# A routed two-layer MLP behind an FFT mixing: where on ScalarE's queue the rows of a later block are asked for

## The chip, the cores and the metric

The kernel runs on one core of one Trainium2 chip. The metric is the time on the device in microseconds (us) of one launch, and the median over several runs is compared. Everything is float32.

## The reference

The input `x` has 8 batches of 2496 rows with 256 columns. Two operations follow each other.

```python
X = np.fft.rfft(x, axis=1)                       # mixing along the rows of a batch
y = np.fft.irfft(X * (filt_r + 1j * filt_i)[None], n=2496, axis=1)

tokens = y.reshape(8 * 2496, 256)                # 19968 rows
expert = token_ids * 2654435761 % 8              # which of 8 experts a row goes to
for e in range(8):
    out[expert == e] = np.maximum(tokens[expert == e] @ w1[e], 0) @ w2[e]
```

`w1[e]` is 256 x 1024 and `w2[e]` is 1024 x 256. The result has one row of 256 for each token, in the order of the tokens.

## The kernel before, in words

**Mixing.** A transform of length 2496 is done as 39 x 64, in products with tables (`wf_t`, `d_t`, `e_t`, `wi_t`) on TensorE (PE). Between the two halves of a transform the data go through DRAM, because rows and columns have to change places. For one batch: `stage1` makes products `pa` (L267), which ScalarE (ACT) copies out of PSUM (L269), and writes `d1` to DRAM (`d<-mid`, L297); `load2` reads it again (`mid<-d`, L303, on the queue of SyncE, SP); `forward` makes `pb` (L312), which VectorE (DVE) multiplies with the filter; `back` makes `pc` (L335), ACT copies it (L338) and writes `d2` (L342, on ACT's queue); `load4` reads it (`t<-d`); `stage3` makes `pd` (L267), ACT copies it (L269), and GpSimd (POOL) scatters the rows to a DRAM buffer `xs` in the order of their experts (L433). The products of the mixing share four PSUM buffers; each is free again when its copy out of PSUM is done.

**Routing.** The rows in `xs` lie in 85 places of 256 rows, called blocks here; every block belongs to one expert. For block `i` the function `step(i)` issues, in this order: the sums of the weights of block `i + 1` on POOL (L877), the scatter of the results of block `i - 1` on POOL (L1014), the first product with its relus (`up`), a load of weights (`w1` of block `i + 2`, on SP), the transposes (DVE L855, which read the rows `xg` of block `i + 1`) and sums for block `i + 1`, the second product (`down`), and another load of weights (`w2` of block `i + 2`).

`up` works by a scheme with seven products of half size instead of eight. Its partial sums lie in the PSUM banks `a`, `b` and `c` (`up_a`, `up_b`, `up_c`, L887). In the order of the code: the first product goes to bank `a`, and ACT copies it into the quarter `h21` of the hidden layer `ht` (L898). After it come products in `b` and `c`; DVE adds them up (L894); ACT applies the relu to the four quarters (L891) as they get ready, the last of them at the end of `up`. `down` makes 32 products `dps` (L922) which read `ht`. After every eighth of them there is a spot, in which pieces of the mixing may be issued.

**How they are interleaved.** A block needs only those batches whose rows it can hold. There are five stages, `STAGES = (2, 3, 4, 6, 8)`: blocks 0 to 9 hold rows of the first two batches alone, blocks 10 to 19 of the first three, blocks 20 to 29 of the first four, blocks 30 to 49 of the first six, and from block 50 on of all. So mixing of batches 2 to 7 is laid between the steps 0 to 49: a list of pieces, each with a due time in steps, written out by hand. `run_until` and `spot` issue all pieces that have become due. From step 50 (`WS`) another form of the step is used, `late_step`, which the change doesn't touch. [...]

**Asking for rows.** `load(j)` (from L835) fetches the rows of block `j` into `xg` with four transfers of 64 KB and their places in the output into `no` with a fifth, of 1 KB; from block 2 on all five are issued on ACT's queue (L844). There are two buffers for `xg`. `ask` decides when a block is fetched:

```python
def ask(i, sooner=False):
    j = asked[0]
    if j <= i + 2 or (sooner and j == i + 3 < NT and stage_of[j] == stage_of[j - 1]):
        if j < NT:
            load(j)
            asked[0] += 1
```

It is called twice in a step: once in `up`, for block `i + 2`, and once in the first spot of `down`, with `sooner`, for block `i + 3`. The second may not cross into a new stage, since the first block of a stage must wait for the scatters of the batches that come with it. So the call in the spot has nearly always done the work already when the next step's `up` comes to its own call. The call in `up` loads something only at the start (step 0 loads block 2) and at the first block of each further stage: step 8 loads block 10, step 18 block 20, step 28 block 30, step 48 block 50.

[...]

Of the kernel before, what the change touches and what calls it, by code (L numbers as in the profile page):

```python
# [125 lines left out]
def kernel(  # L126
# [319 lines left out]
    def weights(i, which):  # L446

        if i >= NT:
            return
        if i >= 2 and which == 0:  # L450
            ws[i] = ws[i - 2][0:2]
        eng, kw = nc.sync, {}
        if which == 0:
            ws[i].append(eng.value_load(chunk_i[0:1, 0, i:i + 1], min_val=0, max_val=E - 1))
            if i >= 2:
                ws[i].append(eng.value_load(chunk_i[0:1, 1, i:i + 1], min_val=0, max_val=1))
        e = ws[i][2]
        if i >= 2:
            kw = {"cond": ws[i][3]}
        if which == 0:  # L460


            for f in (slice(0, F // 2), slice(F // 2, F)) if i < 2 else (slice(0, F),):
                eng.dma_start(out=ws[i][0][:, :, f],
                              in_=moe_w1[bass.ds(e, 1)].rearrange("one (p dp) f -> p (one dp) f", p=P)[:, :, f], **kw)
        else:
            eng.dma_start(out=ws[i][1], in_=moe_w2[bass.ds(e, 1)].rearrange("one (fp p) d -> p (one fp) d", p=P), **kw)
            if WS <= i < NSURE:
                eng.dma_start(out=late["t2"][i % 2].rearrange("p k f c -> p (k f c)"),
                              in_=t2_dram[bass.ds(e, 1)].rearrange("one p k -> p (one k)"), **(kw if i >= WS + 2 else {}))  # L470
# [280 lines left out]
    def chain(k):  # L751

        for step, j in ((Batch.turn2, k + 1), (Batch.back_c, k - 2), (Batch.forward, k)):
            if 0 <= j < N_2:
                step(first, j)
# [79 lines left out]
    def load(i):  # L835

        g = gath.tile([P, TB // 32, C // 4], F32, name=f"xg_{i}", tag="xg")
        no = nums.tile([P, 2], I32, name=f"no_{i}", tag="no")
        rows = xs[tiles[i] * TB:(tiles[i] + 1) * TB, :]
        moves = [(g[32 * q:32 * q + 32, :, :], rows[:, 64 * q:64 * q + 64].rearrange("(a t) c -> t a c", t=32))  # L840
                 for q in range(4)]
        moves.append((no[:].bitcast(F32), rows[:, C:C + 1].rearrange("(h p) c -> p (h c)", p=P)))
        for k, (to, src) in enumerate(moves):
            ld = (nc.sync if i < 2 and (i or k < 3) else nc.scalar).dma_start(out=to, in_=src)  # L844
            for b in range(STAGES[stage_of[i]], B):
                tc.declare_no_dep(ld.ins, group=f"xs_{b}", reason="the tiles of a stage hold tokens of its batches alone")
            if stage_of[i] < G - 1:
                tc.declare_no_dep(ld.ins, group="xs_pad", reason="places without a token lie in the last stage alone")
            tc.add_to_no_dep_group("xs_read", ld.ins)
        xg[i], to_rows[i] = g, no  # L850

    def token_parts(i, to=None):

        xt = work.tile([P, DP, 2, P], F32, name=f"xt_{i}", tag="xt")[:] if to is None else to
        nc.vector.transpose(out=xt.rearrange("p d h (a t) -> p (h a) d t", t=32),  # L855
                            in_=xg[i][:, :, 0:C // 4].rearrange("p a (c d) -> p a d c", d=DP))
        parts[i] = {(h, d): xt[:, d, h, :] for h in range(2) for d in range(DP)}

    def token_sums(i, to=None, which=range(4)):
        x = parts[i]  # L860
        st = parts[i].get("sums", to)
        if st is None:
            st = work.tile([P, 4, P], F32, name=f"st_{i}", tag="st")
        for k in which:
            p, q, op = (((1, 0), (1, 1), OP.add), (0, (0, 0), OP.subtract),
                        ((0, 0), (1, 0), OP.subtract), ((0, 1), 1, OP.subtract))[k]
            p, q = [st[:, v, :] if isinstance(v, int) else x[v] for v in (p, q)]
            nc.vector.tensor_tensor(st[:, k, :], p, q, op=op)
        parts[i]["sums"] = st

    def weight_sums(i, eng=None):

        eng, w1, h = eng or nc.gpsimd, ws[i][0], F // 2
        b11, b12, b21, b22 = [w1[:, d, f * h:f * h + h] for d in range(DP) for f in range(2)]
        t = [tpool[i % 2].tile([P, h], F32, name=f"tw_{i}_{k}", tag=f"tw{k}") for k in range(4)]
        for k, (p, q) in enumerate(((b12, b11), (b22, t[0][:]), (b22, b12), (b21, t[1][:]))):
            eng.tensor_tensor(t[k][:], p, q, op=OP.subtract)  # L877
        sums[i] = t

    def up(i, ht, between=lambda: None):  # L880
        w1, x, st, t = ws[i][0], parts[i], parts[i]["sums"], sums[i]
        ps = {k: banks[k].tile([P, 4, P], F32, name=f"up_{i}_{k}", tag=k) for k in "abc"}
        h11, h12, h21, h22 = [ht[:, h, 4 * f:4 * f + 4, :] for h in range(2) for f in range(2)]

        def product(bank, w, xx, first, fs=range(4)):
            for f in fs:
                nc.tensor.matmul(out=ps[bank][:, f, :], lhsT=w[:, f * P:(f + 1) * P], rhs=xx,  # L887
                                 start=first and f == 0, stop=True, skip_group_check=True)

        def relu(out, in_):  # L890
            nc.scalar.activation(out=out, in_=in_, func=AF.Relu)  # L891

        def plus(out, bank, other):
            nc.vector.tensor_tensor(out, ps[bank][:], other, op=OP.add)  # L894

        h = F // 2
        product("a", w1[:, 0, 0:h], x[0, 0], True)
        nc.scalar.copy(out=h21, in_=ps["a"][:])  # L898
        between()
        product("b", t[1], st[:, 1, :], True)  # L900
        plus(h12, "b", h21)
        product("c", t[0], st[:, 0, :], True)
        plus(h22, "c", h21)
        product("a", w1[:, 1, 0:h], x[0, 1], False, (0, 1))
        product("b", t[2], st[:, 2, :], False)
        plus(h22, "b", h22)
        relu(h22, h22)
        product("a", w1[:, 1, 0:h], x[0, 1], False, (2, 3))
        relu(h11, ps["a"][:])
        product("c", w1[:, 1, h:], st[:, 3, :], False)  # L910
        plus(h12, "c", h12)
        relu(h12, h12)
        product("b", t[3], x[1, 1], False)
        plus(h21, "b", h21)
        relu(h21, h21)
# [95 lines left out]
    def store(i, halves=range(2)):  # L1011
        o = rows[i]
        for h in halves:
            st = nc.gpsimd.indirect_dma_start(  # L1014
                out=out[:], out_offset=bass.IndirectOffsetOnAxis(ap=to_rows[i][:, h:h + 1], axis=0),
                in_=o[:, h, :], in_offset=None, bounds_check=N - 1, oob_is_err=False)
            tc.declare_no_dep(st.ins, group="out_rows", reason="distinct rows")
            tc.add_to_no_dep_group("out_rows", st.ins)
# [9 lines left out]
# [8 lines that stand above are left out]
    def spot(i, k):  # L1036
        if k == 0:
            ask(i, True)
        if k < 3:
            run_until(i + .7 + .1 * k)  # L1040

    def run_until(t):
        while main and main[0][0] < t:
            main.pop(0)[1]()

    def late_step(i):
        ht = work.tile([P, 2, FP, P], F32, name=f"ht_{i}", tag="ht")
        store(i - 1, (1,))
        if i + 1 < NSURE:
            weight_sums(i + 1)  # L1050
        store(i - 1, (0,))
        both(i, ht)

    def step(i):
        if i >= WS:
            late_step(i)
            return
        ht = work.tile([P, 2, FP, P], F32, name=f"ht_{i}", tag="ht")
        if i + 1 < NSURE:
            weight_sums(i + 1)  # L1060
        if i > 0:
            store(i - 1)
        up(i, ht, lambda: ask(i))
        weights(i + 2, 0)
        if i + 1 < NSURE:
            token_parts(i + 1)
            token_sums(i + 1)
        run_until(i + .6)
        down(i, ht, lambda k: spot(i, k))
        weights(i + 2, 1)  # L1070
        run_until(i + 1)
# [59 lines left out]
```

## Time and profile before

| | us |
|---|---|
| median of 3 runs | 1452.11 |
| lowest and highest of these | 1450.68 and 1458.1 |
| the profiled execution | 1424.24 |
| its span in the trace | 1422.5 |
| PE busy | 1373.4 (97%) |
| DVE busy | 890.2 (63%) |
| POOL busy | 830.3 (58%) |
| ACT busy | 416.6 (29%) |
| DMA moved, mean over the span | 196 GB/s |

The profile is one execution on the chip. "Busy" leaves out the instructions that issue DMAs, so an engine whose queue stands at a DMA issue counts as idle. "Idle before, releaser" is the time in which an engine did nothing ahead of an instruction, and what ended it. The chain of waits is followed back from the last instruction: at each step to what released it. The granted clock (PEclk) is the share of its full clock that TensorE got. The profiled execution took 27.87 us less than the median of the runs without a profile.

The requests that the change moves and the copy L898 ahead of them, by the trace of before (us from the start of the span):

| step | copy L898 starts | xg issued from, for | no issued | first relu L891 after it | fetched block |
|---|---|---|---|---|---|
| 0 | 143.96 | 144.18, 5.53 | 151.47 | 151.92 | 2 |
| 8 | 302.80 | 303.17, 1.82 | 305.02 | 306.65 | 10 |
| 18 | 494.07 | 494.68, 5.07 | 500.75 | 501.18 | 20 |
| 28 | 687.25 | 687.54, 1.97 | 689.55 | 691.11 | 30 |
| 48 | 1011.71 | 1012.02, 1.84 | 1013.90 | 1015.70 | 50 |

### The profile page before, as it was taken

To read this page: it belongs to the slowest core of one execution; us is meant where nothing else is said; L and a number is where in the kernel's file an instruction comes from. 1 tells how busy PE (TensorE), PEld (TensorE's weight loads), DVE (VectorE), ACT (ScalarE), POOL (GpSimd) and SP (SyncE) were. 2 spreads that over 40 slices of the span, in tenths; PEclk is the share of its full clock that TensorE was granted. 3 is DMA by queue.
4 is the path that set the end of the run, shared out by engine and by line. 5 is a ranking of instruction groups with operands and counts; after the bars stand their busy time and mean duration, and the time that the engine had idled before them with its cause. 6 is when DMAs were issued, how large, how long until landed. Compare 5 with 4: busy or idle time off the path is not lost.

```text
span 1422.5 us, 26307 instructions
## 1 busy us (share of the span) xinstructions
PE 1373.4 (97%) x9398; PEld 1273.3 (90%) x9398; DVE 890.2 (63%) x1636; ACT 416.6 (29%) x760; POOL 830.3 (58%) x736
## 2 busy tenths in 40 slices
PE   7898999999999999999999999999999999999997
PEld 7776888989888988889999899999999999999997
DVE  7773575575556566445665477657766776676775
ACT  4554122223232223232222222222222222222222
POOL 6167243844665565578533587788855566555563
PEclk9999899999999999999999999999999999999999
DMA  8677765757987698888755785887742526261611
GB/s 222 206 235 216 212 218 121 260 192 245 269 270 224 183 284 264 261 262 273 241 167 131 219 258 170 235 242 235 254 138 68 190 62 199 46 218 42 215 46 35
DMA packets 244505, 278.33 MB, mean 196 GB/s; under 512 B 125171, under 2 KB 213670, under 8 KB 234948
## 3 DMA queue, kind: packets, MB, share of 16 engines
q1 hardware_dynamic: 95149, 179.33, 40.2%
q10 hardware_dynamic: 129303, 52.69, 15.4%
q0 software_dynamic: 19920, 44.59, 8.9%
q8 instruction: 77, 1.26, 0.4%
q14 instruction: 56, 0.46, 0.1%
HBM read 293.65 MB, written 86.15 MB: 267 GB/s over the span
## 4 chain that ended last, share of the span: by engine, by line
PE 86%; DMA 8%; DVE 3%; issue 1%; ACT 1%; ACTq 0%; SPq 0%; POOLq 0%; POOL 0%; DVEq 0%
PE dps L922 22%; PE up_b L887 9%; PE up_a L887 6%; PE up_c L887 6%; PE pd L267 5%; PE pb L312 4%; PE dnc L949 4%; PE dnb L949 4%; PE dna L949 4%; PE upc L944 4%; PE upa L944 4%; PE pc L335 3%; PE pa L267 3%; DMA t<-d 2%; PE upe L944 2%; PE upb L944 2%
## 5 line engine op out<-in xcount | busy, mean ns | idle before, releaser
L922 PE MATMUL dps<-wts,ht 128*128 128x256 f32 x1600 | 370.9, 382 | 6.1 <-ACT ht L891 6.1
L922 PEld LDWEIGHTS dps<-wts,ht 128*128 128x128 f32 x1600 | 304.7, 192 | 50.6 <-ACT ht L891 7.3
L1014 POOL DMA_INDIRECT out_dram<-osb,no x158 | 165.2, 1046 | 219.2 <-DVE osb L956 137.8
L433 POOL DMA_INDIRECT xs<-o,sidx x176 | 177.0, 1006 | 168.7 <-ACT o L269 73.3
L877 POOL TENSOR_TENSOR tw<-wts 128x512 f32<-128x512 f32 x158 | 205.1, 1298 | 116.0 <-DMA wts<-in_moe_w_dram 92.4
L877 POOL TENSOR_TENSOR tw<-wts,tw 128x512 f32<-128x512 f32 x158 | 206.1, 1305 | 6.2
L894 DVE TENSOR_TENSOR ht<-up_b,ht 128x512 f32<-128x512 f32 x150 | 103.7, 691 | 114.6 <-PE up_b L887 91.2
L891 ACT ACTIVATE ht<-ht 128x512 f32<-128x512 f32 x150 | 94.3, 630 | 188.8 <-DVE ht L894 164.9
L322 DVE TENSOR_TENSOR z<-pb,filt 64x512 f32<-64x512 f32 x160 | 110.2, 689 | 30.9 <-PE pc L335 28.9
L927 DVE COPY osb<-dps 128x512 f32<-128x512 f32 x50 | 34.6, 691 | 150.2 <-PE dps L922 149.7
L887 PE MATMUL up_a<-xt,wts 128*128 128x128 f32 x800 | 115.3, 277 | 9.1 <-DVE xt L855 4.9
L887 PEld LDWEIGHTS up_a<-xt,wts 128*128 128x128 f32 x800 | 105.9, 193 | 12.7 <-DVE xt L855 5.3
L887 PE MATMUL up_b<-st,tw 128*128 128x128 f32 x800 | 107.4, 278 | 2.7 <-DVE ht L894 1.8
L887 PEld LDWEIGHTS up_b<-st,tw 128*128 128x128 f32 x800 | 98.1, 193 | 4.9 <-issue 3.7
L953 ACT ACTIVATE ht<-ht 128x512 f32<-128x512 f32 x90 | 56.6, 630 | 122.1 <-DVE ht L956 75.8
L894 DVE TENSOR_TENSOR ht<-up_c,ht 128x512 f32<-128x512 f32 x100 | 69.0, 690 | 37.2 <-PE up_c L887 32.4
L338 ACT COPY mid<-pc 128x512 f32<-128x512 f32 x60 | 35.0, 584 | 154.8 <-PE pc L335 91.5
L267 PE MATMUL pd<-t,wi_t 120*117 120x256 f32 x320 | 77.5, 385 | 2.6 <-DMA t<-d 2.6
L318 DVE TENSOR_TENSOR y<-pb,filt 128x512 f32<-128x512 f32 x80 | 55.1, 689 | 37.8 <-PE pb L312 35.6
L269 ACT COPY o<-pd 117x512 f32<-117x512 f32 x80 | 45.0, 585 | 104.4 <-DMA xg<-xs 45.4
L312 PE MATMUL pb<-mid,d_t 128*128 128x256 f32 x280 | 74.1, 388 | 1.1 <-DVE z L322 1.1
L898 ACT COPY ht<-up_a 128x512 f32<-128x512 f32 x50 | 29.3, 587 | 150.6 <-PE up_a L887 120.7
(210 smaller groups left out, 2466.1 us busy)
## 6 DMA issues: line engine op xcount, KB each, us to landing
wts<-in_moe_w_dram SPq DMA_DIRECT2D x162, 1024.0 KB
xg<-xs ACTq DMA_DIRECT2D x321, 64.0 KB
mid<-d SPq DMA_DIRECT2D x70, 256.0 KB
d<-mid ACTq DMA_DIRECT2D x60, 256.0 KB
d_t<-t2s SPq DMA_DIRECT2D x15, 1024.0 KB
e_t<-t2s SPq DMA_DIRECT2D x15, 1024.0 KB
x<-in_x_dram SPq DMA_DIRECT2D x39, 312.0 KB
t<-d SPq DMA_DIRECT2D x12, 960.0 KB
```

The costliest lines, as they stand in the source:

```text
L267: nc.tensor.matmul(out=ps[0:cols * H, k, :], lhsT=w[:], rhs=src[:, 2 * i + k, :], start=True, stop=True)
L312: nc.tensor.matmul(out=ps[:, i, :], lhsT=d_t[:, s, :], rhs=rhs, start=True, stop=True)
L322: nc.vector.tensor_tensor(out=z[b], in0=ps[a], in1=f_t[1][64 * hi:64 * hi + 64, s1:s1 + 2, :], op=OP.mult)
L433: st = nc.gpsimd.indirect_dma_start(out=xs[:], out_offset=bass.IndirectOffsetOnAxis(ap=index, axis=0), in_=rows, in_offset=None, bounds_ch ...
L877: eng.tensor_tensor(t[k][:], p, q, op=OP.subtract)
L887: nc.tensor.matmul(out=ps[bank][:, f, :], lhsT=w[:, f * P:(f + 1) * P], rhs=xx, start=first and f == 0, stop=True, skip_group_check=True)
L891: nc.scalar.activation(out=out, in_=in_, func=AF.Relu)
L894: nc.vector.tensor_tensor(out, ps[bank][:], other, op=OP.add)
L922: nc.tensor.matmul(out=ps[:, h, :], lhsT=ht[:, h, fp, :], rhs=w2[:, fp, :], start=(fp == 0), stop=(fp == FP - 1))
L944: nc.tensor.matmul(out=ps[:, f, :], lhsT=w[:, f * P:(f + 1) * P], rhs=xx, start=first and f == 0, stop=True, skip_group_check=True)
L949: nc.tensor.matmul(out=ps[:, 0, :], lhsT=a[:, f, :], rhs=b[:, f, :], start=first and f == 0, stop=True, skip_group_check=True)
L1014: st = nc.gpsimd.indirect_dma_start(out=out[:], out_offset=bass.IndirectOffsetOnAxis(ap=to_rows[i][:, h:h + 1], axis=0), in_=o[:, h, :], i ...
```

## The change

The parameter `between` of `up` goes away, and with it the call of `ask` behind the copy L898. `step` calls `ask(i)` itself when `up` has been issued. On ACT's queue the five transfers of a request so stand behind the four relus of `up` and ahead of whatever the mixing issues on ACT next. Instructions below line 898 up to the call move up by one line: `dps` is L921 in the changed kernel, `DVE L894` is L894 still, and the copy L898 stays at its number.

```diff
-    def up(i, ht, between=lambda: None):
+    def up(i, ht):
...
         product("a", w1[:, 0, 0:h], x[0, 0], True)
         nc.scalar.copy(out=h21, in_=ps["a"][:])
-        between()
         product("b", t[1], st[:, 1, :], True)
         plus(h12, "b", h21)
...
-        up(i, ht, lambda: ask(i))
+        up(i, ht)
+        ask(i)
         weights(i + 2, 0)
```

## The prediction

> **What bounds the kernel now.** I begin with the page's chain of waits and its row for the product that follows the relus. The columns of the row are busy time, mean ns of one, then PE's idle time just ahead of it and what ended it.
>
> ```profile
> PE 86%; DMA 8%; DVE 3%; issue 1%; ACT 1%; ACTq 0%; SPq 0%; POOLq 0%; POOL 0%; DVEq 0%
> L922 PE MATMUL dps<-wts,ht 128*128 128x256 f32 x1600 | 370.9, 382 | 6.1 <-ACT ht L891 6.1
> ```
>
> PE sets the end, and all of the 6.1 us that it ever waited ahead of dps was for ACT's relus. The waits say how often (total us, times, longest), and what held ACT itself:
>
> ```profile
> PE dps L922 <- ACT ht L891: 6.1, 2, 3.1
> ACT ht L891 <- DMA xg<-xs: 14.0, 3, 7.4
> ACT mid L338 <- DMA xg<-xs: 26.0, 6, 9.0
> ```
>
> The 6.1 us are two waits, not fifty. They lie in step 0 and step 18. ACT's timeline at step 0 and step 18 shows them (start, length, what, idle time before):
>
> ```profile
> 143.96 0.59 ACT L898 COPY ht<-up_a 128x512 f32<-128x512 f32 x1 [6.35 <-PE up_a L887]
> 144.18 5.53 ACTq L844 DMA_DIRECT2D xg<-xs  x4
> 151.47 0.40 ACTq L844 DMA_DIRECT2D no<-xs  x1
> 151.92 0.63 ACT L891 ACTIVATE ht<-ht 128x512 f32<-128x512 f32 x1 [7.37 <-DMA xg<-xs]
> ...
> 494.68 5.07 ACTq L844 DMA_DIRECT2D xg<-xs  x4
> 500.75 0.38 ACTq L844 DMA_DIRECT2D no<-xs  x1
> ```
>
> The relu stands behind the request in ACT's order, so it waits till the fifth transfer (`no`) is issued. PE's timeline has dps at 153.09 after 3.12 us idle, and at 502.35 after 3.00 us. Then the granted clock halves; by windows (last three columns: PEclk, DMA share, GB/s):
>
> ```profile
> 150.00:152.00 2.00, 0.00 (x0) 0.00 (x0) 1.93 (x5) 0.08 (x1) 0.00 (x0) 1.00 0.34 70
> ...
> 152.00:154.00 2.00, 0.91 (x2) 0.82 (x3) 0.37 (x2) 2.00 (x4) 0.00 (x0) 0.52 0.59 133
> 154.00:156.00 2.00, 2.00 (x6) 1.55 (x6) 0.00 (x0) 0.07 (x1) 0.00 (x0) 0.50 1.02 317
> 158.00:160.00 2.00, 2.00 (x9) 1.69 (x8) 0.00 (x0) 0.00 (x0) 0.00 (x0) 0.78 0.93 285
> ```
>
> The third place to look is after the second request of a stage, asked in `spot`, which is not moved. At step 8/9:
>
> ```profile
> 312.27 0.33 ACTq L297 DMA_DIRECT2D d<-mid  x1
> 314.37 5.09 ACTq L844 DMA_DIRECT2D xg<-xs  x4
> 320.83 0.38 ACTq L844 DMA_DIRECT2D no<-xs  x1
> 321.26 0.59 ACT L338 COPY mid<-pc 128x512 f32<-128x512 f32 x1 [9.02 <-DMA xg<-xs]
> ```
>
> ACT stands still for 9.02 us here, yet PE loses nothing: its pc product, which needs the PSUM buffer that this L338 frees, starts at 322.65. ACT's copy ends at 321.85, so the cover is 0.80 us.
>
> [...] half clock for 6.83 us from 152.1 and 3.41 us from 503.6. [...] 3.00 us did it, and so did one of 2.03 us (at 238.22, half clock for 3.41 us from 240.8), while one of 1.98 us at 789.39 did not. [...] `xg` landed about 1.9 us after its issue at 303.17, but 7.3 us after that at 144.18, where SP's 1.6 MB of d<-mid were under way.
>
> **The change, part by part.** Nothing is added or removed; PE, DVE, POOL and SP keep their order. `ask` inside `up` has something to load only in steps 0, 8, 18, 28 and 48 (blocks 2, 10, 20, 30, 50); elsewhere the spot of the step before has asked. So 25 issues on ACT's queue (5 x 5) go from ahead of four relus to behind them, ahead of the L338, L269, L342, L297 of the mixing. [...] The `xg` moved are read by DVE L855 only in the next step, so their own later landing costs nothing (the cover is the rest of the step, over 10 us).
>
> Clock price: step 0's 32 dps took 10.02 us against 7.07 us in a step at full clock, so its two half-clock windows cost 2.95 us; after 502.35 dps x8, pb x4 and pd x8 took 2.56 + 1.91 + 2.21 against 1.89 + 1.03 + 1.89, so its one window cost 1.87 us.
>
> *Step 0/1.* Gone: 3.12 + 2.95 = 6.07 us. New: the fourth xg_2 now waits for the first of SP's mid<-d (L303, issued from 151.48, landing about 155, estimated), xg_3's for the third to sixth, landing about 157 to 160.4 (issues of 0.95 us each, 7.63 us for 8). ACT would be free at about 161; before it was at 155.6. PE, 6 us earlier, reaches the block-1 product that needs copy L898 (before: 164.09) at about 158.1; the copy takes 0.59 us. So PE waits about 161.3 - 158.65 = 2.65 us, plus one half-clock window, 1.87. Net gain 6.07 - 4.52 = 1.55. Bounds: +6 if mid<-d lands early or the counter frees before; 0 with two windows or a later release.
>
> *Step 8/9.* No PE wait before (the relu waited 3.27 us, but DVE was ready only at 306.62), so nothing to win. Five issues of about 0.46 us (303.17 to 305.5) move ahead of L338, L342, L269, L297: 2.3 us. d<-mid L297 (983 KB, 312.27, landed about 322.0) goes out at about 314.7. In the new allocation `no` of block 11 waits for that very transfer, landing at 324 to 326.6: ACT free at about 325.7 instead of 321.2. pc then starts at about 325.7 + 0.59 + 0.1 = 326.4 instead of 322.65: 3.75 us, plus one window, 1.87: loss 5.62. Bounds: 0 (it lands by 322), 3.75 + 1.2 + 2.95 = 7.9 with two windows and the latest landing.
>
> *Step 18/19.* Gone: 3.00 + 1.87 = 4.87. New: no_20 waits for a t<-d (about 507.5), xg_21 for a mid<-d (about 509) and an x<-in_x (about 511.3). ACT free at about 512 (before 510.31), while PE, 4.9 us earlier, wants the PSUM buffer that L269 frees at about 510: 2.2 us, and a window in about half the cases, 0.9. Net gain 1.75. Bounds: 0 to 4.87.
>
> *Step 28/29 and 48/49.* No PE wait before (relus at 691.11 and 1015.70 had waited for DVE). xg_31 now waits for w1 of block 30 and x<-in_x, ACT free at about 700.2 instead of 696.6, copy L898 at 702.14 slips by 0.9, with 0.6 of slack: loss 0.3 (0 to 2). At 48/49, ACT is free at about 1024.8, just ahead of L898 at 1025.07: 0 (0 to 1).
>
> Sum: 1.55 - 5.62 + 1.75 - 0.3 = **2.6 us slower**. Against the profiled execution of 1424.24 us (span 1422.5 and 1.74 around it) that is 1426.8. The median shown is 1452.11, 27.87 above; I carry the difference over: 1454.7.
>
> **Rivals.**
>
> *A: both waits stay won.* ACT is free whenever it is wanted next; gain 6.07 + 4.87 = 10.9, less 0.3: 1441.5. For it: PE's 3.12 and 3.00 us have one cause, which is gone, and landing times above are estimates. Against it: DMA is at 1.02 of its share at 154 to 158, just when the moved requests go out, and ACT already stood 9.02 us behind one of them. Most that can be won, whatever else.
>
> *B, the other side: ACT is held behind the 983 KB write of step 8.* pc waits for the release, and the clock falls for two windows: 7.9. Steps 1 and 19 get longer waits as well: step 1 nets +0.5 (6.07 - 2.65 - 2.95, a second window), step 19 nets -0.6 (4.87 - 2.2 - 1.4 - 1.87: a release 1.4 us later and the whole window), steps 29 and 49 lose 3 together. Sum 11.0 slower: 1463.1. It decides from the point where no_11 is issued after about 326, 4 us past the old landing of the write. For it: every stretch concerned moves 219 to 322 GB/s, so a write that starts 2.3 us later can end more than 2.3 us later. Against it: its landing is the only long one, and POOL and DVE don't slip.
>
> *C: nothing is gained or lost.* The two waits come back as equal waits a block later, and no_11's counter is free in time: 0, 1452. For it: in both places the release I work out is a transfer's landing, which doesn't depend on where the request stands. Against it: it needs 10.9 us of new waits at steps 1 and 19, where I find 4.52 + 3.1 = 7.6.
>
> **How the numbers follow.** A measurement of this kernel can tell about 0.5% from no change, 7.3 us, so 1444.8 to 1459.4 is "same". My own case has 0.45, of which 0.05 lies beyond 1459.4 (bounds of step 8/9 and 28/29 together); A 0.13; B 0.35[...]; C 0.07. Faster 0.13, same 0.40 + 0.07 = 0.47, slower 0.40. The range reaches from near A to past B: 1443 to 1470. The likeliest: 1455.
>
> **What would show it.** Right: no PE gap ahead of dps (L921 after) at 150 and 499, full clock there; an ACT wait of several us ahead of L338 or L269 near 321 to 326, ended by no, xg or d<-mid, and a new PE gap at pc; a PE gap of 2 to 3 us near 155 to 161 at up_b or up_a for L898 and near 505 to 512 for L269. Wrong: PE gapless through 300 to 330 (step 8/9 costs nothing: then A); the gap at dps still there (C); gaps away from the five places, which I can't derive from the order of the issues.

## The result, and the profile after

The changed kernel takes 1460.97 us (median of 20 runs, 1454.7 to 1471.99), the kernel before 1455.1 us in 20 runs beside it (1449.15 to 1465.71). The ratio is 1.0045 (95% interval 1.0025 to 1.0065): about 6.5 us slower, just short of the 0.5% that the prediction took as the least difference that can be told. A second set of runs of the same kernel gave 1.0043 (1.0023 to 1.0062).

The later sets of runs were each on another chip, and the kernel before takes 1458 and 1453 us on two of these chips and 1423 us on the other two; the profile of before that the prediction was read from (1424.24 us) fits the second kind, the result and the profile of after (1460.99 us) the first, so the two spans, 1422.5 and 1459.2 us, must not be subtracted. Step 0 alone starts 8.9 us later in the trace of after, and nothing ahead of step 0 was changed. For a trace of the first kind I profiled the kernel before again (`e1_before_again`, below); every ratio here is against runs of before in the same set. Both timings of the changed kernel itself are from chips of the first kind.

From the page of after, the chain of waits and the row of the product that follows the relus:

```profile
PE 76%; DMA 9%; DVE 6%; issue 3%; ACTq 1%; ACT 1%; another core or an unknown queue 1%; POOL 1%; SPq 1%; POOLq 0%; DVEq 0%
L921 PE MATMUL dps<-wts,ht 128*128 128x256 f32 x1600 | 368.8, 381 | 0.0
```

The 6.1 us ahead of dps are gone to the last tenth. Two lines from the waits of after (total us, times, longest):

```profile
PE up_a L887 <- ACT ht L898: 10.8, 5, 4.8
ACT mid L338 <- DMA xg<-xs: 39.8, 8, 12.2
```

ACT stands longer behind requests ahead of L338, 39.8 us where it was 26.0. The 10.8 us at up_a are no mark of the change as a whole: in the first profile of before they are 4.2 us, but in the second one 11.2 (experiment 1). Only 0.37 us in step 1 and 1.83 us in step 29 lie at the places where a request was moved.

**Step 0/1.** In ACT's timeline of after the relu starts when DVE is ready, and the request comes behind it. Now it is the copy L898 of step 1 that stands behind the request.

```profile
157.81 0.63 ACT L891 ACTIVATE ht<-ht 128x512 f32<-128x512 f32 x1 [4.38 <-DVE ht L894]
160.21 2.26 ACTq L844 DMA_DIRECT2D xg<-xs  x4
165.38 0.39 ACTq L844 DMA_DIRECT2D no<-xs  x1
168.61 0.59 ACT L898 COPY ht<-up_a 128x512 f32<-128x512 f32 x1 [7.93 <-DMA xg<-xs]
```

The 32 dps take 7.07 us at full clock, and the new wait is at the place that was worked out, only smaller: PE stands 0.37 us ahead of up_a, where 2.65 us were predicted.

**Step 8/9.** ACT's timeline of after:

```profile
325.27 0.59 ACT L338 COPY mid<-pc 128x512 f32<-128x512 f32 x1 [2.04 <-DMA xg<-xs]
330.52 0.33 ACTq L297 DMA_DIRECT2D d<-mid  x1
331.37 4.71 ACTq L844 DMA_DIRECT2D xg<-xs  x4
340.15 0.38 ACTq L844 DMA_DIRECT2D no<-xs  x1
340.57 0.59 ACT L338 COPY mid<-pc 128x512 f32<-128x512 f32 x1 [12.25 <-DMA xg<-xs]
```

PE's timeline has the three products that waited:

```profile
327.53 1.10 PE L312 MATMUL pb<-mid,d_t 128*128 128x256 f32 x4 [0.51 <-issue]
332.79 1.10 PE L312 MATMUL pb<-mid,d_t 128*128 128x256 f32 x4 [1.57 <-DVE z L322]
341.21 1.13 PE L335 MATMUL pc<-y,e_t 128*128 128x256 f32 x4 [2.13 <-ACT mid L338]
```

The write L297 issued at 330.52 landed at 340.13, and `no` of block 11 was issued 0.02 us later. In the trace both signal their landing on the same semaphore, called a counter here. The 893 transfers of SP's and ACT's queues in the trace of before signal on eight of these, which makes 885 pairs of neighbours on a counter. In the 691 pairs for which the first one's landing is recorded in full, the second was issued behind it each time, in 62 of them by 0.03 us or less, and no stretch between two issues holds the marks of more than one landing (in after 437 pairs, 31 of them by so little). In before, `no` of block 11 came next on its counter to a `mid<-d` of SP, which landed at 320.81, and was issued at 320.83; in after the write stands in that place. That is the hold that the prediction names, and the 2.13 us at pc are its price.

The 0.51 and 1.57 us at pb were not foreseen. The first L338 starts 2.04 us late, behind the five issues, but that is not what PE waited for: this L338 ended at 325.86, and PE came to the first of the two late pb only at 327.02. DVE's timeline of after has what ended just ahead of both:

```profile
326.04 1.39 DVE L322 TENSOR_TENSOR z<-pb,filt 64x512 f32<-64x512 f32 x2
331.26 1.39 DVE L322 TENSOR_TENSOR z<-pb,filt 64x512 f32<-64x512 f32 x2 [1.90 <-PE pc L335]
```

These L322, which read the pb ahead, end at 327.43 and 332.65, and the late pb start 0.10 and 0.14 us after that. The built program says why. Which of the four PSUM buffers a product gets is fixed when the program is built. In the kernel before, the first of the two gets the buffer that L338 empties and the second one that L269 empties; in the changed kernel both get the buffer of the pb directly ahead of them, so PE waited until DVE had read it.

**Step 18/19.** The wait ahead of dps is gone, and the wait for L269 that the prediction puts in its place is not in the trace. In step 19 PE waits 2.59 us at up_b; in the same step of experiment 1 it waits 1.76 us at up_b and 1.17 us at up_c, so this need not come from the change.

**Step 28/29.** ACT's timeline of after:

```profile
724.05 1.82 ACTq L844 DMA_DIRECT2D xg<-xs  x4
727.41 4.70 ACTq L844 DMA_DIRECT2D xg<-xs  x4
732.90 0.59 ACT L338 COPY mid<-pc 128x512 f32<-128x512 f32 x1 [8.46 <-DMA xg<-xs]
735.55 0.59 ACT L898 COPY ht<-up_a 128x512 f32<-128x512 f32 x1 [2.07 <-issue]
```

PE's timeline has the product that waits for the copy:

```profile
736.19 0.71 PE L887 MATMUL up_a<-xt,wts 128*128 128x128 f32 x4 [1.83 <-ACT ht L898]
```

The copy L898 of step 29 comes 17.8 us after that of step 28; with the request of step 28 in front it is 14.9 us in every trace.

### The profile page after: what moved, and what is told of

Same layout as the page of the kernel before. It is cut to its first block, busy times and chain, and to the rows that moved or that the text cites. A ratio compares the mean times of both kernels' runs of the same rounds, so it can differ in the third digit from the quotient of the medians.

```text
span 1459.2 us, 26306 instructions
## 1 busy us (share of the span) xinstructions
PE 1387.4 (95%) x9398; PEld 1281.4 (88%) x9398; DVE 871.7 (60%) x1636; ACT 415.4 (28%) x760; POOL 829.1 (57%) x736
## 4 chain that ended last, share of the span: by engine, by line
PE 76%; DMA 9%; DVE 6%; issue 3%; ACTq 1%; ACT 1%; another core or an unknown queue 1%; POOL 1%; SPq 1%; POOLq 0%; DVEq 0%
PE dps L921 17%; PE up_b L887 8%; PE up_a L887 5%; PE up_c L887 5%; PE dnc L948 4%; PE pd L267 4%; PE dna L948 4%; PE dnb L948 4%; PE upc L943 3%; PE upa L943 3%; PE pa L267 3%; PE pb L312 3%; PE pc L335 3%; DMA xg<-xs 2%; PE upe L943 2%
## 5 line engine op out<-in xcount | busy, mean ns | idle before, releaser
L921 PE MATMUL dps<-wts,ht 128*128 128x256 f32 x1600 | 368.8, 381 | 0.0
L921 PEld LDWEIGHTS dps<-wts,ht 128*128 128x128 f32 x1600 | 303.3, 191 | 44.1 <-issue 1.2
L894 DVE TENSOR_TENSOR ht<-up_b,ht 128x512 f32<-128x512 f32 x150 | 103.7, 691 | 133.6 <-PE up_b L887 72.7
L887 PE MATMUL up_a<-xt,wts 128*128 128x128 f32 x800 | 117.3, 280 | 16.3 <-ACT ht L898 10.8
L322 DVE TENSOR_TENSOR z<-pb,filt 64x512 f32<-64x512 f32 x160 | 110.2, 689 | 34.4 <-PE pc L335 31.0
L894 DVE TENSOR_TENSOR ht<-up_c,ht 128x512 f32<-128x512 f32 x100 | 69.0, 690 | 46.9 <-PE up_c L887 29.8
L338 ACT COPY mid<-pc 128x512 f32<-128x512 f32 x60 | 35.1, 584 | 161.3 <-PE pc L335 86.9
L269 ACT COPY o<-pd 117x512 f32<-117x512 f32 x80 | 44.4, 586 | 105.0 <-PE pd L267 50.9
L898 ACT COPY ht<-up_a 128x512 f32<-128x512 f32 x50 | 29.4, 588 | 157.6 <-PE up_a L887 68.5
```

The costliest lines, as they stand in the source:

```text
L322: nc.vector.tensor_tensor(out=z[b], in0=ps[a], in1=f_t[1][64 * hi:64 * hi + 64, s1:s1 + 2, :], op=OP.mult)
L921: nc.tensor.matmul(out=ps[:, h, :], lhsT=ht[:, h, fp, :], rhs=w2[:, fp, :], start=(fp == 0), stop=(fp == FP - 1))
```

## The experiments

Short diffs are against the kernel named. "Front" means behind the copy L898 and ahead of the relus, as in the kernel before; "behind" means behind the relus, as in the changed one.

**1. The kernel before again** (no edit).

> The kernel before, unchanged, for a second trace: the profiled execution of before took 27.9 us less than the median of its runs, so its stretches may not be typical. If that profile is an outlier through the clock and the timing of transfers in all parts alike, this one has a span near 1450 and the time is lost in many small places (some of it ahead of step 0, at 144 us). The two relu waits at step 0 and step 18 (3.12 and 3.00 us ahead of dps) should be there again if they come from the order of the issues; if they were chance, they are gone or much smaller. Time ratio 1.000, and the width of its interval says what can be told at all.

Measured: ratio 1.0005 (0.9976 to 1.0034), span of the profiled execution 1459.2 us. The relu waits ahead of dps are there again, 1.32 us at step 0 and 3.20 us at step 18. The waits of this trace, for comparison with after:

```profile
PE up_a L887 <- ACT ht L898: 11.2, 6, 4.8
PE dps L922 <- ACT ht L891: 4.5, 2, 3.2
```

All of PE's gaps over 0.2 us sum to 65.7 us, where the first profile had 39.8: the difference lies ahead of step 0 (7.2 us), in steps 2 to 8 (5.3), 19 to 22 (5.9) and 24 to 28 (3.8), nearly all of it where the change moves nothing.

**2. Behind at steps 0 and 18 alone.**

```diff
-        up(i, ht, lambda: ask(i))
+        behind = i in (0, 18)
+        up(i, ht, (lambda: None) if behind else (lambda: ask(i)))
+        if behind:
+            ask(i)
```

> Only the requests of steps 0 and 18, which cost PE a wait in the profile of before, stand behind the relus; 8, 28 and 48 as before. My theory (the loss lies at steps 8/9, the gain at 0 and 18): no PE gap ahead of dps at either place, a smaller new one in steps 1 and 19 (my working: net 1.5 to 1.75 us won at each), so 3 us or 0.2% faster than before, at most 10. Rival (the waits come back a block later in full): ratio 1.000. Rival (any move shifts the later transfers for the worse): slower by 3 us or more, with new gaps away from steps 0/1 and 18/19.

Measured: ratio 0.9992 (0.9969 to 1.0014). There is no gap ahead of dps; there are new gaps of 2.08 us at step 1 (up_a) and in step 19 of 1.20 us (up_a), 2.30 and 1.88 us (pd). The time is 0.08% lower where 0.2% was expected; the interval holds both that and no change, so the gain isn't shown.

**3. Behind at steps 8, 28 and 48 alone** (the same edit with `(8, 28, 48)`).

> Only the requests of steps 8, 28 and 48, which cost PE nothing in the profile of before, stand behind the relus; 0 and 18 as before. My theory: slower by some 6 us (0.4%), with PE gaps of 2 to 5 us in all at steps 8/9 (pb, pc) and up to 2 us at 28/29, ACT standing 10 us or more ahead of an L338 at 8/9, nothing at 48/49; the relu waits at 0 and 18 are there as before. Rival (the loss of the changed kernel lies at 0/1 and 18/19): ratio 1.000 and no gaps at 8/9.

Measured: ratio 1.0045 (1.0024 to 1.0065), as much as the whole change. Steps 8 to 10 take 48.6 us instead of 43.9 in the kernel before (experiment 1), steps 28 to 30 take 40.0 instead of 35.1. Step 48 to 49 takes 13.2 us in both. The rival falls: the loss is in steps 8 and 28, where PE waited for nothing before. One thing was not as expected: the relu wait is there at step 0 (2.15 us), but not at step 18, though the request stands in front in both.

**4. The changed kernel without the second request in the spot** at the five steps.

```diff
-        if k == 0:
+        if k == 0 and i not in (0, 8, 18, 28, 48):
             ask(i, True)
```

> The changed kernel, but the first spot of steps 0, 8, 18, 28 and 48 asks for nothing: the second block of the stage is asked for by the next step, behind its relus, where ask has something to load again. It tells whether ACT's standing behind the second request is what costs. My theory: ACT is no longer held ahead of L338, L269 and L898 at steps 8/9, 18/19, 0/1 and 28/29, so the PE gaps there (4.1 us at 8/9, 2.6 at 18/19, 1.8 at 28/29 in the changed kernel) go, and the kernel is 5 to 10 us faster than the changed one, level with before or up to 5 us faster. Rival (the 2.3 us by which the five issues delay the mixing's own writes is what costs): the gaps at 8/9 stay at 3 us or more. Rival (the requests are late then): waits ahead of up_a for DVE's transposes in steps 2, 10, 20, 30, 50.

Measured: ratio 1.006 (1.003 to 1.009), so it is not faster than the changed kernel. In the kernel that ran, the request so put off stood in front of the relus of the next step, not behind them as the expectation has it. The long hold is gone and with it the gap at pc; the copy L898 of step 29 comes after 14.9 us again. But the 2.1 us at pb stay (the first rival had 3 us or more), step 29 got a new gap of 1.91 us at pb, and dps waits 1.13 us for a relu in step 49. My expectation of 5 to 10 us less than the changed kernel did not come true: without the hold the loss is as large, and it lies elsewhere.

**5. The counter at step 8/9.** The changed kernel, with the 1 KB `no` of block 11 asked for together with block 10, so that the later transfers come to other counters (shortened):

```diff
...
+        if i == 10:
+            early[11] = nums.tile([P, 2], I32, name="no_11", tag="no")
+            moves.append((early[11][:].bitcast(F32), xs[...block 11...]))
```

> The changed kernel, but the 1 KB transfer no of block 11 goes out together with the request of block 10, so that the request of block 11 is four transfers, none of which shares its completion counter with the 983 KB write d<-mid (L297). If the hold of ACT at step 8/9 (12.25 us, no_11 issued 0.02 us after that write landed, PE gap of 2.13 us at pc) comes from the shared counter, ACT is released some 4 us earlier, right after the second mid<-d has landed and about 4 to 5 us after L297, and the gap at pc is gone; the gaps of 0.48 and 1.54 us at pb, which I put down to the five issues ahead of L338, stay. Rival (the hold is the crowded DMA in general): ACT is released as late as before, the pc gap stays near 2 us. Time: some 2 us less than the changed kernel, 4 us more than before, hardly to be told.

Measured: ratio 1.0019 (1.0002 to 1.0037) against before, on a chip on which before takes 1423 us. ACT's timeline of this kernel:

```profile
315.90 0.35 ACTq L297 DMA_DIRECT2D d<-mid  x1
316.34 5.61 ACTq L850 DMA_DIRECT2D xg<-xs  x4
321.99 0.58 ACT L338 COPY mid<-pc 128x512 f32<-128x512 f32 x1 [6.43 <-DMA d<-mid]
```

ACT is free 6.1 us after the write was issued, 1 us more than I expected but before the write landed (322.80); in the changed kernel it was 10.05 us, and the write had landed. So the hold by the write comes with the shared counter: without it, L338 started 0.81 us ahead of the landing. The gap at pc is gone too, but that proves nothing: on this chip the write landed 6.9 us after its issue and not 9.6, and even with the shared counter L338 would have ended at about 323.8 (my estimate: the landing, then 1.0 us for `no` and L338 as in after), ahead of PE, which comes to pc at 324.23. The two gaps at pb stay, 0.51 and 1.57 us to the hundredth, and at step 29 PE waits 2.10 us for the copy L898: these two losses are there on such a chip as well.

**6. The request of step 8 behind the mixing's pieces.** The kernel before, with

```diff
         run_until(i + .6)
+        if i == 8:
+            ask(i)
         down(i, ht, lambda k: spot(i, k))
```

and no request in `up` at step 8.

> The kernel before, but the request of step 8 stands behind the pieces of the mixing that are due ahead of the second product (L338, L342, L269, L297), directly ahead of the second request. If the pb gaps (0.48 and 1.54 us) come from the five issues ahead of L338, they are gone. The fourth xg_10 now shares its counter with the write L297 itself, and block 11's xg with xg_10: by the counters ACT is held until the write has landed and xg_10 after it, some 24 to 26 us after the copy L898 of step 8, and pc (free at about 20 us) waits 3 to 6 us. So step 8/9 is slower still than in the changed kernel, though the requests are hardly later. Rival (only the issues ahead of L338 matter): step 8 takes 22.7 us again.

Measured: ratio 1.0013 (0.9988 to 1.0038). ACT's timeline of this kernel, then the pc product from PE's:

```profile
310.60 8.80 ACTq L844 DMA_DIRECT2D xg<-xs  x4
324.34 0.38 ACTq L844 DMA_DIRECT2D no<-xs  x1
324.76 0.59 ACT L338 COPY mid<-pc 128x512 f32<-128x512 f32 x1 [14.79 <-DMA xg<-xs]
```

```profile
325.40 2.08 PE L335 MATMUL pc<-y,e_t 128*128 128x256 f32 x4 [4.86 <-ACT mid L338]
```

The pb gaps are gone. In the built program every product has the PSUM buffer of the kernel before again. In the changed kernel and in experiments 3, 4, 5 and 10, which have the request of step 8 directly behind the relus on ACT's queue, the two pb have the buffer of the pb ahead, and all their traces have the gaps of 0.51 and 1.57 us; no other trace has them. The hold has grown: the fourth `xg` was issued 0.02 us after the write L297 landed (319.02), and `no` of block 11 as soon as that `xg` had landed (324.32). ACT is free 24.2 us after the copy L898 of step 8, as the counters say, and PE waits 4.86 us at pc; steps 8 to 9 take 28.7 us. So the gaps at pb and the hold come apart: this kernel has the hold alone, experiment 5 the pb gaps alone.

**7. The ten requests of the five places on POOL's queue.** The changed kernel, with (shortened)

```diff
+            eng = nc.gpsimd if i in (2, 3, 10, 11, 20, 21, 30, 31, 50, 51) else ...
+            ld = eng.dma_start(out=to, in_=src)
```

> The changed kernel, but the ten requests of blocks 2, 3, 10, 11, 20, 21, 30, 31, 50 and 51 are issued on POOL's queue instead of ACT's. If ACT's standing behind requests is the whole cause, none of the waits is left: no relu wait ahead of dps at 0 and 18, no gaps for L338, L269, L898 at 8/9, 19 and 28/29: 3 to 8 us faster than before (ratio 0.995 to 0.998), 9 to 14 faster than the changed kernel. Rival (POOL is held by the same requests instead, and with it the weight sums L877 and the scatters L433 behind them): new PE gaps at up_b for L877, or later xs rows: ratio 1.00 or above. Rival (the transfers themselves are late in these places, whatever queue): about level with before.

Measured: ratio 0.9982 (0.9967 to 0.9997), and in a second set:

> The ten requests on POOL's queue once more, for a second interval: the first was 0.9982 (0.9967 to 0.9997) on the chip on which the kernel before takes 1423 us. If ACT's queue is the cause, the waits ahead of dps, pb, pc and up_a at the five places are gone here too and the ratio is 0.995 to 0.999, on whichever chip. If it was the faster chip's transfers alone that kept the other waits small, the ratio is 1.000 on the slower one.

Measured there: 0.9979 (0.996 to 0.9999), 1418.63 us against 1422.8. In both traces there is no gap at dps, pb or pc at the five places; steps 8 to 9 take 22.7 us, 28 to 29 take 14.9, 18 to 20 take 40.3. In step 1 PE waits 2.65 and 3.90 us for a transfer of `x` ahead of pa. ACT's timeline of the second run shows the place at step 8, and then POOL's, with the two requests:

```profile
313.72 0.33 ACTq L297 DMA_DIRECT2D d<-mid  x1
318.25 0.59 ACT L338 COPY mid<-pc 128x512 f32<-128x512 f32 x1 [4.56 <-PE pc L335]
```

```profile
308.31 2.43 POOL L845 DMA_DIRECT2D xg<-xs  x4
311.41 2.36 POOL L845 DMA_DIRECT2D xg<-xs  x4
```

ACT waits for PE alone, and POOL gets both requests out in one go. Both sets were on chips on which before takes 1423 us, so what the others would show wasn't measured, and this gain can't be added to the 0.45%.

**8. POOL's queue for steps 0 and 18 alone**, the kernel before otherwise (the same edit with blocks 2, 3, 20, 21).

> The kernel before, but only the requests of blocks 2, 3, 20 and 21 (steps 0 and 18, the two places where a request in front costs PE a wait) are on POOL's queue; the others stay in front on ACT's. If the two relu waits and the hold of L269 at 18/19 are worth what the traces show (1.3 to 3.1 us at 0, 3 us at 18, and the half clock behind them), 4 to 8 us faster than before: ratio 0.995 to 0.997. Rival (what is won at 0 and 18 is waited for again between steps 2 and 28, where transfers of the mixing set the pace): 0.999 to 1.000, with longer gaps at pd, pa or pb there.

Measured: ratio 0.9983 (0.9961 to 1.0004). The waits ahead of dps are gone, and at 18 to 20 nothing comes in their place (40.7 us); at step 1 PE waits 2.7 us for `x` ahead of pa instead. The gain is about 2.4 us, not 4 to 8, and its interval reaches 1.000. It settles neither side.

**9. The changed kernel again, beside two others.**

> The changed kernel once more. On the chip of the last runs the kernel before took 1422.7 us, on the one of the first runs 1457.6; the changed kernel was timed on the slower one alone (ratio 1.0045). My theory: the losses at 8/9 (4.4 us there) and 28/29 (2.6 us) and the small gains at 0 and 18 come from the order of issues and the counters, so they are there on either chip: 4 to 5 us lost at steps 8 to 10, 2 to 3 at 28 to 30, and where the chip is the faster one, 2 to 5 us won at 0 to 2 and 18 to 20. Ratio 1.000 to 1.003 on the faster chip, 1.003 to 1.006 on the slower. Rival (the loss is a matter of the slow chip's transfers): no gap at pb, pc or up_a in 8/9 and 28/29 and a ratio below 1 on the faster chip.

Measured: ratio 1.0043 (1.0023 to 1.0062), before at 1453.38 us. The pb gaps are there to the hundredth (0.51, 1.57); the one at pc is not, since ACT was free at 341.9 and pc wanted the buffer at 343.27. At 28/29 the gap is 3.50 us. In all four traces in which `no` of block 11 shares its counter with the write (after, this one and experiments 3 and 10), it is issued 0.02 us after the write has landed; the write takes 9.6, 7.2, 9.1 and 6.9 us, and the gap at pc is 2.13, 0, 1.23 and 0 us. So the hold at 8/9 costs 0 to 2.1 us by the landing of one transfer, the pb gaps always 2.1.

In the same set, behind at steps 0 and 18 alone once more (experiment 2):

> Only the requests of steps 0 and 18 behind the relus, once more, beside the changed kernel on the same chip. My theory: the difference to the changed kernel is what 8, 28 and 48 cost, some 6 to 8 us (0.4 to 0.55%); against before 0 to 5 us are won, more on the faster chip, where step 18 to 20 took 41.4 us in a kernel with the request behind and 43.1 and 45.1 us in two with it in front. Rival (the moves add up otherwise): level with the changed kernel.

Measured: 0.999 (0.9967 to 1.0013). The changed kernel is 0.53% slower than this one in the same set (1.0043 against 0.999), 7.7 us: the price of steps 8, 28 and 48. Beside before, it again can't be told from no change.

**10. The request of block 30 alone on POOL's queue**, the changed kernel otherwise.

> The changed kernel, but the request of block 30 alone is issued on POOL's queue. Then ACT has no first request at step 28, and the counters of xg_31 wait for older transfers alone, no longer for xg_30 and x (landed 6 us after their issue, behind 1 MB of w1). If that is what holds ACT at 28/29 (8.5 us ahead of L338, the copy L898 of step 29 17.8 us after that of step 28 instead of 14.9, PE gap 1.8 to 2.7 us at up_a), ACT is free within 3 us of asking for block 31, the copy comes 14.9 to 15.4 us after the one before, and the gap is gone or under 0.5 us. Rival (the second request is held by the crowd of transfers behind w1 as such): the copy is late by 2 us or more still.

Measured: ratio 1.0008 (0.9988 to 1.0028), some 0.35% or 5 us below the changed kernel in the same set. ACT's timeline of this kernel:

```profile
729.74 1.83 ACTq L845 DMA_DIRECT2D xg<-xs  x4
733.58 0.59 ACT L338 COPY mid<-pc 128x512 f32<-128x512 f32 x1 [3.83 <-PE pc L335]
737.93 0.59 ACT L899 COPY ht<-up_a 128x512 f32<-128x512 f32 x1 [3.76 <-PE up_a L888]
```

ACT waits for PE again, the copy comes 14.9 us after the one before, and the gap at up_a is gone. What had held ACT: in the changed kernel the third `xg` of block 31 shares its counter with an `xg` of block 30, issued at 724.40, behind the 1 MB of w1 (722.28), and landed only at 730.76; it was issued at 730.78. In front of the relus block 30's five transfers are out ahead of w1 (719.90 to 721.97 against 724.16 in experiment 1), and those of block 31 follow one another without a hold (726.31 to 729.17).

## Why the prediction was right, and which terms were off

The time lies in the range and moved to the side of my own case: 0.45% slower where I had 0.18%, and rival B 0.76%. The mechanism was right in part, and that the sum came so close is luck to a good part: the term that was to decide was too large, and the terms that cost most were left out or put near nothing. The table sets the sum beside the traces from chips on which before takes 1453 to 1458 us, each number the time from the copy L898 of one step to that of another, front less behind (positive is a gain). Front is the mean of the traces of before (experiment 1) and of experiments 2, 3 and 9 where they leave the place alone; behind is the mean of the two of the changed kernel and of experiments 2, 3, 9 and 10 where they have it.

| place | predicted | front | behind | difference |
|---|---|---|---|---|
| 0 to 2 | +1.55 | 40.0 (2 traces) | 39.5 (5) | +0.5 |
| 8 to 10 | -5.62 | 43.6 (3) | 47.6 (4) | -4.0 |
| 18 to 22 | +1.75 | 101.1 (2) | 99.9 (5) | +1.2 |
| 28 to 30 | -0.3 | 35.1 (3) | 39.4 (3) | -4.3 |
| 48 to 49 | 0 | 13.2 (3) | 13.5 (4) | -0.3 |
| sum | -2.6 | | | -6.9 |

The sum of the differences, 6.9 us, agrees with the 6.5 us timed. The places at 0 and 18 vary by several us between traces with the same order. The gain at 0 to 2 hangs on one trace (35.3 us in experiment 10; the other four have 39.2 to 41.4), so neither of the two small gains is shown.

*Right.* Wherever the request stands behind, the waits ahead of dps at 0 and 18 are gone, and nearly all of it is given back: at step 18 to 20 behind is 3.4 us ahead (46.7 against 50.1), and from 20 to 22 it loses 2.2 of them. At step 1 the new wait at up_a is there in four of the five traces (0.37 to 2.77 us); a wait for L269 at 18/19 is named in none. The step that was to decide, ACT held at 8/9 by the write L297 through the counter of `no` 11, happened as written in all four traces that could have it, and in experiment 5 ACT no longer waited for the write. Rival A (both waits stay won) falls with 1.0045; C falls as well, since the loss lies at places where nothing was to be won. B's mechanism is there, but it was too dear: a hold of 7.9 us at pc, where 0 to 2.13 was seen; its share of 0.35 was an estimate.

*Off, the makeup of step 8/9.* The prediction compared the counters of the two programs, transfer by transfer, and took all else as equal ("Nothing is added or removed"). The PSUM buffers were not: two pb got the buffer of the pb ahead of them, and this costs 2.1 us in every trace with the request of step 8 behind the relus on ACT's queue. Why the program is built with other buffers once the request stands there stays open. The hold was over-sized in return (3.75 us against 0 to 2.13): PE, held at pb, came 2.1 us late to pc itself, the write landed early in two of the traces, and the stretch at half clock (1.87 us) did not come: the clock stayed at 1.00 after the gap of 2.13 us. So 4.0 us stand where 5.6 were worked out, for other reasons in the main.

*Off, step 28/29, the term that was mis-sized most.* I took 0.3 us with a bound of 2; 4.3 were measured. I had xg_31 wait for w1 and x, as its first two transfers did, and put ACT's release at about 700.2, 12.9 us after the copy L898 of step 28. In after it was 15.1 us. The term left out is that the third transfer of the second request waits for the landing of one of the first. That first request, issued 6.3 us after the copy L898 instead of 0.3, now goes out behind the megabyte of w1, and the transfer in question takes 6.4 us to land instead of 4.3 (experiment 1). After it the two writes L342 still stand ahead of the copy. Experiment 10, which takes the first request off ACT's queue, has the copy on time.

*Off, the base.* I carried the 27.87 us between the profiled execution and the median over as a constant, as if profiling had made the kernel faster. But that profile fits the chips on which before takes 1423 us: against the trace of experiment 1 it lacks 25.9 us of PE gaps out of 36.7 us of span. I could have asked why one execution lies so far below all of its runs.

## What to carry to other kernels

When requests are moved on an engine's queue, price two things apart: the issues themselves, against the next work on that engine that another engine waits for (here L338 came 2.04 us late and still ended before PE wanted its buffer), and what each moved transfer waits for before it is issued, since what stands behind it on that engine waits along (here `no` of block 11 was issued 0.02 us after the write had landed, and L338 behind it came after 12.25 us without work on ACT). Then compare the two built programs in all that is given out in order, buffers as well as counters: here two products got another PSUM buffer, and that cost 2.1 us of PE each time. Where an engine issues transfers and also computes, look for a place where its requests go out at once, or for another engine with slack: here POOL, 58% busy, issued the two requests of step 8/9 from 308.31 to 314.48, and the waits on both sides of the move were gone except in step 1 (2.65 and 3.90 us). And ask whether a profile is one of the usual executions before its base is used: the median beside it tells.

## What the runs showed of the hardware that was not expected

- The same kernel takes 1423 us on two chips and 1453 and 1458 us on two others, with PE products of the same length (dps 382 and 381 ns in the two pages); in the two traces of before, PE's gaps make up 25.9 of the 36.7 us. Each chip was used at one time only, so chip and time can't be told apart, and what makes the gaps longer stays open.
- A PE gap's effect on the clock is not a matter of its length alone: after 2.13 us (step 8/9 in after) the clock stayed full, after 2.67 us (28/29 in experiment 3) it was at 0.50, and in the first profile of before after 2.04 us too.
